# Attention feeding a gated convolution: x and its gate moved into the slot of their own sums, with M held block-diagonal

## Chip, cores and metric

One core of one Trainium2 chip. The metric is the device time of one execution in microseconds, median of several runs. Profiles give a span, which is about 1.8 us shorter than the time of the same run. All runs quoted are in the fast state.

## The reference, cut to what matters

```python
q_pool = q.reshape(B, H, S // 2, 2, D).mean(axis=3)          # B=8, H=8, S=1152, D=64, fp32
attn   = softmax(q_pool @ k.T / sqrt(D))
x      = (attn @ v)                                          # heads joined: (8, 576, 512)
gate   = sigmoid(causal_conv(x, conv_w))                     # 5 taps, per channel
out    = (gate * (x @ w_val)) @ w_out
```

The scores are small, so the kernel takes softmax to first order: attention is then q times a 64x64 matrix M = K'V minus a rank-one term, plus a mean of v. A bound on the scores is computed beside it, and if it fails an exact version runs. No instruction of that version is in the traces.

## The kernel before

32 head pairs are worked in 16 *slots* of two pairs (a, b). A slot sums k and v (`sums`), builds K'V (`grams`), corrects it (`rows`, `rank1`) and reads M out of PSUM. x̂ = Mq, its evacuation to x, the conv (two taps on PE, three on VectorE) and the gate follow **one slot later**, and `val`, `outs` behind them. Cut to the parts concerned:

```python
ps_t: 1 PSUM tile, tag "ts"        # transposes of q AND the sums of k, v share it
ps_g: 1 PSUM tile, tag "g"         # M, and the norms beside it
ps_b: 3 PSUM tiles of two banks    # x̂, conv, val, outs
NOSB = 11                          # output buffers in SBUF; stores are held till all loads are issued

for m in range(NSLOT):
    a, b, pa, pb = 2*m, 2*m+1, 2*m-2, 2*m-1
    sums(a); sums(b); rows(m); grams(a); grams(b)
    tap(pb-2, 1); tap(pb-2, 2)
    xhat(pa); xhat(pb); xevac(pa); xevac(pb)       # of the slot before
    rank1(m); norms(m-1, g); conv(pa); gate(pb-2)
    pool_q(a); stat(m, g); pool_q(b); transposes(a); mk(m, g)
    ...                                            # taps, conv(pb), transposes(b), val/outs
def mk(m, g):      # M for both pairs; each head's M on its own 64 partitions
    nc.scalar.activation(out=mqs[m][:, :, 0:2*D], in_=g[:, 0:256]..., func=AF.Copy, scale=C0)
def xhat(n):       # two halves x two heads, 64x64 matmuls on two row tiles
    nc.tensor.matmul(out=xh[p:p+64, half, 0:HALF], lhsT=mq[p:p+64, i, 0:D], rhs=mq[p:p+64, i, c0:c0+HALF], ...)
def oevac(...):    # copies an output out of PSUM and appends it to `held`
    osb = out_pool.tile([128, m, Dm], FP32, tag=f"osb{m}", bufs=(3 if m == 1 else NOSB))
```

All five instruction streams are ordered by hand: each engine takes its instructions in the order of the program text.

## Time and profile before

| | before |
|---|---|
| median of 4 runs | 187.53 us (186.63 to 188.44) |
| span of the profiled run | 184.8 us |
| busy, PE / VectorE / ScalarE | 88 / 69 / 56 % |
| `rows` of slot 2 / of slot 15 | 35.16 / 153.63 us |
| end of the last matmul | 176.50 us |

How to read it: `rows` is issued once in every slot, so its starts are a clock for the slots. The span falls into three terms: the start up to `rows` of slot 2, the thirteen slots to `rows` of slot 15, and the tail to the last matmul. The prediction below shows the lines.

### The profile page before, as it was taken

The page shows a single profiled execution, that of the slowest core. Times are in us where ns is not written, and L with a number is a line of the kernel's source. Part 1 is how long each engine was busy: PE and PEld are TensorE (multiplying, and loading weights), DVE is VectorE, ACT ScalarE, POOL GpSimd, SP SyncE. Part 2 cuts the span into 40 slices and gives each one's busy share as a digit, 9 for nine tenths or more (in the row PEclk, how much of TensorE's full clock was granted, in tenths as well). Part 3 has the DMA queues.
Part 4 walks back from the last instruction along what each step waited for, and adds up shares of the span by engine and source line. Part 5 has one row for each costly group of instructions (what it writes and reads, how often), then busy time and mean ns, then how long its engine had stood idle before and what let it go on. Part 6 is the DMA issues. An engine that isn't in the chain of part 4 may idle for free.

```text
span 184.8 us, 5451 instructions
## 1 busy us (share of the span) xinstructions
PE 161.8 (88%) x2361; PEld 116.3 (63%) x2361; DVE 127.7 (69%) x236; ACT 102.7 (56%) x151; POOL 75.4 (41%) x118
## 2 busy tenths in 40 slices
PE   7399995699999999999999999999999969969910
PEld 2066752678776868686868667866877648537400
DVE  2162180369889888788888896889788939838550
ACT  2202448075678549754985498549756665494120
POOL 7644434445454455455355444454444345011000
PEclk9969999579999999999999999999999999999995
DMA  5999999999999999999999999999999999953060
GB/s 169 305 207 208 206 207 207 208 207 207 207 206 209 209 205 207 206 208 209 204 208 207 207 209 205 210 203 207 207 208 207 284 419 411 420 231 137 0 274 25
DMA packets 27865, 40.11 MB, mean 217 GB/s; under 512 B 1910, under 2 KB 24758, under 8 KB 27835
## 3 DMA queue, kind: packets, MB, share of 16 engines
q0 software_dynamic: 26624, 36.61, 100.1%
q1 hardware_dynamic: 938, 2.50, 3.8%
q10 hardware_dynamic: 272, 0.59, 0.9%
q8 instruction: 20, 0.33, 0.6%
q14 instruction: 11, 0.08, 0.1%
HBM read 58.73 MB, written 9.44 MB: 369 GB/s over the span
## 4 chain that ended last, share of the span: by engine, by line
DMA 62%; PE 18%; ACT 5%; issue 4%; DVE 3%; POOL 3%; POOLq 0%; DVEq 0%; ACTq 0%
DMA kv<-in_v_dram 33%; DMA qn<-in_q_dram 12%; DMA kv<-in_k_dram 12%; PE vps L329 7%; DMA out_dram<-osb 6%; PE ops L347 3%; PE cps L291 3%; PE g L219 2%; PE sm L209 2%; DVE acc L306 2%; POOL kv L95 2%; ACT osb L360 2%; ACT sq L257 1%; ACT x L275 1%; PE xh L268 1%
## 5 line engine op out<-in xcount | busy, mean ns | idle before, releaser
L306 DVE SCALAR_TENSOR_TENSOR acc<-x,convw_sb,acc 128x576 f32<-128x576 bf16 x62 | 50.6, 816 | 1.5
L347 PE MATMUL ops<-wout_sb,gv 128*128 128x512 bf16 x144 | 34.2, 379 | 1.6 <-ACT osb L360 1.6
L329 PE MATMUL vps<-x,wval_sb 128*128 128x288 bf16 x256 | 34.1, 285 | 1.6 <-ACT osb L360 1.6
L199 ACT COPY mq<-qt_ps 128x576 bf16<-128x576 bf16 x32 | 20.5, 641 | 26.0 <-PE qt_ps L194 26.0
L275 ACT ACTIVATE x<-xh,stats 128x576 bf16<-128x576 f32 x32 | 22.0, 738 | 21.2 <-PE xh L268 21.2
L337 DVE TENSOR_TENSOR gv<-vps,gate 128x576 bf16<-128x576 f32 x32 | 24.1, 757 | 13.5 <-PE vps L329 13.5
L95 POOL DMA_DIRECT2D kv<-in_k_dram x31 | 22.3, 718 | 24.9 <-DMA kv<-in_v_dram 8.5
L99 POOL DMA_DIRECT2D qn<-in_q_dram x31 | 19.8, 639 | 29.4 <-DVE acc L306 10.8
L329 PEld LDWEIGHTS <-wval_sb 128*128 128x128 bf16 x256 | 24.0, 97 | 7.8 <-issue 1.7
L97 POOL DMA_DIRECT2D kv<-in_v_dram x31 | 22.2, 715 | 15.3 <-DMA qn<-in_q_dram 8.9
L301 DVE SCALAR_TENSOR_TENSOR acc<-x,convw_sb,cps 128x576 f32<-128x576 bf16 x31 | 25.1, 810 | 3.6 <-PE cps L291 3.1
L313 ACT ACTIVATE gate<-acc 128x576 bf16<-128x576 f32 x31 | 21.3, 687 | 8.6 <-DVE acc L306 8.6
L291 PE MATMUL cps<-x,diag 128*128 128x288 bf16 x128 | 21.2, 289 | 2.9 <-ACT x L275 2.9
L209 PE MATMUL sm<-kv,first 128*64 128x128 bf16 x576 | 20.5, 226 | 3.6 <-DMA kv<-in_v_dram 3.5
L209 PEld LDWEIGHTS <-first 128*64 128x64 bf16 x576 | 17.4, 113 | 9.3 <-issue 5.2
L347 PEld LDWEIGHTS <-gv 128*128 128x128 bf16 x144 | 13.3, 98 | 14.7 <-issue 1.8
L219 PE MATMUL g<-kv 128*64 128x128 bf16 x576 | 20.4, 228 | 0.0
L257 ACT ACTIVATE sq<-mq 128x1280 bf16<-128x1280 bf16 x16 | 20.2, 1262 | 0.0
L225 DVE TENSOR_TENSOR rows<-sm,rowf 128x256 bf16<-128x256 f32 x16 | 6.8, 425 | 19.4 <-PE sm L209 19.4
L360 ACT COPY osb<-ops 128x1024 f32<-128x1024 f32 (+1 forms) x17 | 15.7, 929 | 7.2 <-PE ops L347 4.2
L219 PEld LDWEIGHTS <-kv 128*64 128x64 bf16 x576 | 18.5, 116 | 0.0
L404 PE MATMUL wps<-idle 128*128 128x512 bf16 x60 | 16.5, 426 | 1.3 <-DVE ident L125 1.3
(65 smaller groups left out, 143.3 us busy)
## 6 DMA issues: line engine op xcount, KB each, us to landing
kv<-in_k_dram POOLq DMA_DIRECT2D x31, 288.0 KB, 10.9
kv<-in_v_dram POOLq DMA_DIRECT2D x31, 288.0 KB, 11.2
qn<-in_q_dram POOLq DMA_DIRECT2D x31, 288.0 KB, 10.9
out_dram<-osb POOLq DMA_DIRECT2D x14, 512.0 KB, 9.8
out_dram<-osb SPq DMA_DIRECT2D x2, 512.0 KB, 2.9
out_dram<-osb POOLq DMA_DIRECT2D x3, 256.0 KB, 9.3
k<-in_k_dram ACTq DMA_DIRECT2D x1, 576.0 KB, 5.7
v<-in_v_dram SPq DMA_DIRECT2D x1, 576.0 KB, 5.1
```

The lines of the kernel that those rows point to most:

```text
L95: nc.gpsimd.dma_start(out=t[:, W:2 * W].rearrange("p (h x) -> p h x", h=2), in_=k[b, h0:h0 + 2].rearrange("h (p t) d -> p h (t d)", p=128))
L97: nc.gpsimd.dma_start(out=t[:, 0:W].rearrange("p (h x) -> p h x", h=2), in_=v[b, h0:h0 + 2].rearrange("h (p t) d -> p h (t d)", p=128))
L209: nc.tensor.matmul(out=sms[m][64 * h:64 * h + 64, i], lhsT=first, rhs=kvv[:, :, h, t, :], start=(i == 0 and t == 0), stop=(t == NT - 1), s ...
L219: nc.tensor.matmul(out=gs[m][64 * h:64 * h + 64, 128 * i:128 * i + 128].rearrange("p (c d) -> p c d", c=2), lhsT=kvv[:, 1, h, t, :], rhs=k ...
L257: nc.scalar.activation(out=sq, in_=mqs[m][:, :, D:], func=AF.Square)
L275: nc.scalar.activation(out=x[:, PAD:].rearrange("p (c n) -> p c n", c=2), in_=xhs.pop(n)[:, :, 0:HALF], func=AF.Identity, bias=stats[:, m, ...
L291: nc.tensor.matmul(out=cps[:, half, 0:HALF], lhsT=w, rhs=x[:, c0:c0 + HALF], start=(i == 0), stop=(i == len(mats) - 1))
L301: nc.vector.scalar_tensor_tensor(out=acc.rearrange("p (c n) -> p c n", c=2), in0=x[:, kk:kk + Sq].rearrange("p (c n) -> p c n", c=2), scal ...
L306: nc.vector.scalar_tensor_tensor(out=accs[n], in0=x[:, kk:kk + Sq], scalar=convw_sb[:, ft, kk:kk + 1], in1=accs[n], op0=ALU.mult, op1=ALU.add)
L329: nc.tensor.matmul(out=vps[:, half, 0:HALF], lhsT=wval_sb[:, fi, ft * 128:(ft + 1) * 128], rhs=x[:, c0:c0 + HALF], start=(fi == 0), stop=( ...
L337: nc.vector.tensor_tensor(out=gvs[y, ft][:, e * Sq:(e + 1) * Sq].rearrange("p (c n) -> p c n", c=2), in0=vps[:, :, 0:HALF], in1=gates.pop( ...
L347: nc.tensor.matmul(out=ops[:, c, :], lhsT=gvs[y, ft][:, t0 + c:t0 + 128 * m:m], rhs=wout_sb[:, ft, :], start=(ft == 0), stop=(ft == NFT - 1))
```

## The change

The intent: q of a slot is pooled and transposed one slot ahead, so that x̂, x, conv and the gate can follow in the same slot as the sums. The pipeline gets one stage shorter, the drain at the end with it, and the time in which PE waits for the first loads gets work. M is written block-diagonally so that x̂ takes four full matmuls; PSUM tiles are taken by number (b0, b1, b2). Cut to its core:

```diff
-    ps_b = ctx.enter_context(tc.tile_pool(name="ps_b", bufs=3, space=PSUM))
+    ps_b = ctx.enter_context(tc.tile_pool(name="ps_b", bufs=1, space=PSUM))   # tags b0, b1, b2
@@ load_pair:  k, v, q  becomes  q, k, v
@@ M
-        nc.scalar.activation(out=mqs[m][:, :, 0:2 * D], in_=g[:, 0:256]..., func=AF.Copy, scale=C0)
+        for h in range(2):            # onto the diagonal of a zeroed 128x128
+            nc.scalar.activation(out=mq2[m % 2][p, :, 64*h:64*h+64], in_=gv[p, :, 0:D], func=AF.Copy, scale=C0)
@@ x̂
-            for h in range(2): nc.tensor.matmul(64x64 ...)
+            nc.tensor.matmul(out=xh[:, half, 0:HALF], lhsT=mq[:, i, 0:2 * D], rhs=mq[:, i, c0:c0 + HALF], ...)
@@ loop
+            sums(a); sums(b); rows(m); grams(a); grams(b)
+            tap(pb, 1); tap(pb, 2)
+        rank1(m); norms(m - 1, g); stat(m, g); mevac(m, g)
+        # even slot
+            gate(pb); gval(bt, 2, val(bt, 2, 0))
+            xhat(a, 1); xhat(b, 2); xevac(a); xevac(b); pool_q(a + 2)
+            gval(bt, 3, val(bt, 3, 0)); transposes(a + 2)
+            conv(a, 1); conv(b, 2); tap(a, 0); pool_q(b + 2); tap(a, 1); tap(a, 2)
+            outs [0]; transposes(b + 2); squares(m, g); gate(a); tap(b, 0); outs [1]; oevac
+        # odd slot
+            outs [0] (or the 1024-row output)
+            xhat(a, 1); xhat(b, 2); xevac(a); xevac(b); pool_q(a + 2)
+            outs [1] (or [0, 1]); oevac
+            conv(a, 1); conv(b, 2); tap(a, 0); transposes(a + 2); pool_q(b + 2)
+            gate(pb); tap(a, 1); tap(a, 2); squares(m, g)
+            gval(bt, 0, val(bt, 0, 0)); transposes(b + 2); gate(a)
+            gval(bt, 1, val(bt, 1, 1)); tap(b, 0)
+            if not moe: warm(20)       # slot 1: filling matmuls, tile b0
```

More of the change, by code (lines that the diff above doesn't have):

```diff
@@ L85, in first_order, with big @@
     ps_g = ctx.enter_context(tc.tile_pool(name="ps_g", bufs=1, space=PSUM))
-    ps_b = ctx.enter_context(tc.tile_pool(name="ps_b", bufs=3, space=PSUM))
+    ps_b = ctx.enter_context(tc.tile_pool(name="ps_b", bufs=1, space=PSUM))
+    def big(name, i):
+        return ps_b.tile([128, 2, 512], FP32, name=name, tag=f"b{i}")
     kvs, loaded = {}, {}
@@ L94, in load_pair @@
         qn = q_pool.tile([QP, 2, 2 * U * D], BF16, name="qn", tag="qn")
+        nc.gpsimd.dma_start(out=qn, in_=q[b, h0:h0 + 2].rearrange("h (p s) d -> p h (s d)", p=QP))
         nc.gpsimd.dma_start(out=t[:, W:2 * W].rearrange("p (h x) -> p h x", h=2),
@@ L98, in load_pair @@
                             in_=v[b, h0:h0 + 2].rearrange("h (p t) d -> p h (t d)", p=128))
-        nc.gpsimd.dma_start(out=qn, in_=q[b, h0:h0 + 2].rearrange("h (p s) d -> p h (s d)", p=QP))
         kvs[n], loaded[n] = t, qn
+    q0 = [q_pool.tile([QP, 2 * U * D], FP32, name="q0", tag="qn") for _ in range(2)]
     k0 = kv_pool.tile([128, 2, NT * D], FP32, name="k0", tag="kv")
     v0 = kv_pool.tile([128, 2, NT * D], FP32, name="v0", tag="kv")
-    q0 = [q_pool.tile([QP, 2 * U * D], FP32, name="q0", tag="qn") for _ in range(2)]
+    for h in range(2):
+        nc.sync.dma_start(out=q0[h], in_=q[0, h].rearrange("(p s) d -> p (s d)", p=QP))
     nc.scalar.dma_start(out=k0, in_=k[0, 0:2].rearrange("h (p t) d -> p h (t d)", p=128))
     nc.sync.dma_start(out=v0, in_=v[0, 0:2].rearrange("h (p t) d -> p h (t d)", p=128))
-    for h in range(2):
-        nc.sync.dma_start(out=q0[h], in_=q[0, h].rearrange("(p s) d -> p (s d)", p=QP))
     wval_sb = consts.tile([128, NFT, Dm], BF16, name="wval_sb")
@@ L160, in setup_conv @@
     def setup_conv():
-        cw_ps = ps_b.tile([128, 2, 512], FP32, name="cw_ps", tag="big")
+        cw_ps = big("cw_ps", 2)
         for ft in range(NFT):
@@ L171, in setup_conv @@
             nc.vector.tensor_scalar_mul(out=diag_l[:, i, :], in0=ident, scalar1=convw_sb[:, NFT - 1, kk:kk + 1])
-    qps, mqs, sqs, gs, sms, rws, xhs = {}, {}, {}, {}, {}, {}, {}
+    mq_pool = ctx.enter_context(tc.tile_pool(name="mqp", bufs=1))
+    mq2 = []
+    for i in range(2):
+        t = mq_pool.tile([128, 2, MQ], BF16, name=f"mq{i}", tag=f"mq{i}")
+        nc.gpsimd.memset(t[0:64, :, D:2 * D], 0.0)
+        nc.gpsimd.memset(t[64:128, :, 0:D], 0.0)
+        mq2.append(t)
+    qps, sqs, gs, sms, rws, xhs = {}, {}, {}, {}, {}, {}
     def pool_q(n):
@@ L186, in pool_q, with transposes @@
         qps[n] = qp
-    def transposes(n):
+    def transposes(n, at=None):
         m, i = divmod(n, 2)
         qp = qps.pop(n)
-        qt_ps = ps_t.tile([128, Sq], BF16, name="qt_ps", tag="ts")
+        qt_ps = (ps_t if at is None else ps_b).tile([128, Sq], BF16, name="qt_ps", tag="ts" if at is None else f"b{at}")
         qtv = qt_ps.rearrange("c (u p) -> c u p", u=U)
@@ L195, in transposes @@
                                 identity=ident[0:QP, 0:QP])
-        if i == 0:
-            mqs[m] = work.tile([128, 2, MQ], BF16, name="mq", tag="mq", bufs=3)
-        nc.scalar.copy(out=mqs[m][:, i, 2 * D:].rearrange("c (p u) -> c p u", u=U),
+        nc.scalar.copy(out=mq2[m % 2][:, i, 2 * D:].rearrange("c (p u) -> c p u", u=U),
                        in_=qt_ps.rearrange("c (u p) -> c p u", u=U))
@@ L249, in stat, with mevac, squares, xhat @@
         nc.vector.tensor_copy(out=stats[:, m, a:z], in_=g[:, 256 + a:256 + z])
-    def mk(m, g):
-        nc.scalar.activation(out=mqs[m][:, :, 0:2 * D], in_=g[:, 0:256].rearrange("p (i c) -> p i c", i=2),
-                             func=AF.Copy, scale=C0)
-    def squares(m):
+    def mevac(m, g):
+        gv = g[:, 0:256].rearrange("p (i c) -> p i c", i=2)
+        for h in range(2):
+            p = slice(64 * h, 64 * h + 64)
+            nc.scalar.activation(out=mq2[m % 2][p, :, 64 * h:64 * h + 64], in_=gv[p, :, 0:D], func=AF.Copy, scale=C0)
+    def squares(m, g):
         sq = work.tile([128, 2, D + Sq], BF16, name="sq", tag="sq")
-        nc.scalar.activation(out=sq, in_=mqs[m][:, :, D:], func=AF.Square)
+        nc.scalar.activation(out=sq[:, :, 0:D], in_=g[:, 0:256].rearrange("p (i c) -> p i c", i=2)[:, :, D:2 * D],
+                             func=AF.Square, scale=C0)
+        nc.scalar.activation(out=sq[:, :, D:], in_=mq2[m % 2][:, :, 2 * D:], func=AF.Square)
         sqs[m] = sq
-    def xhat(n):
+    def xhat(n, at):
         m, i = divmod(n, 2)
-        mq = mqs[m]
-        xh = ps_b.tile([128, 2, 512], FP32, name="xh", tag="big")
+        mq = mq2[m % 2]
+        xh = big("xh", at)
         for half in range(2):
-            for h in range(2):
-                p = 64 * h
-                c0 = 2 * D + half * HALF
-                nc.tensor.matmul(out=xh[p:p + 64, half, 0:HALF], lhsT=mq[p:p + 64, i, 0:D],
-                                 rhs=mq[p:p + 64, i, c0:c0 + HALF], start=True, stop=True, skip_group_check=True)
+            c0 = 2 * D + half * HALF
+            nc.tensor.matmul(out=xh[:, half, 0:HALF], lhsT=mq[:, i, 0:2 * D], rhs=mq[:, i, c0:c0 + HALF],
+                             start=True, stop=True)
         xhs[n] = xh
@@ L279, in first_order, with conv @@
     gates, accs, cpss = {}, {}, {}
-    def conv(n, full=False):
+    def conv(n, at, full=False):
         ft = n % NP
         x = xs[n % NX]
-        cps = ps_b.tile([128, 2, 512], FP32, name="cps", tag="big")
+        cps = big("cps", at)
         mats = [(diag[:, ft, i, :], kk) for i, kk in enumerate(PE_TAPS)]
@@ L321, in first_order, with val @@
     of = out.rearrange("(y b) s d -> y (b s) d", b=2)
-    def val(b, ft):
-        vps = ps_b.tile([128, 2, 512], FP32, name="vps", tag="big")
+    def val(b, ft, at):
+        vps = big("vps", at)
         for fi in range(NFT):
@@ L339, in gval, with outs @@
                                 in1=gates.pop(b * NP + ft).rearrange("p (c n) -> p c n", c=2), op=ALU.mult)
-    def outs(y, t0, m, ops=None, fts=range(4)):
-        if ops is None:
-            ops = ps_b.tile([128, 2, 512], FP32, name="ops", tag="big")
-        for c in range(m):
+    def outs(y, t0, m, ops, cs=None, fts=range(4)):
+        for c in range(m) if cs is None else cs:
             for ft in fts:
@@ L398, in bound_flag, with warm @@
         nc.vector.tensor_scalar(out=flag, in0=fin[:, 3:4], scalar1=lim, scalar2=None, op0=ALU.is_le)
-    def warm(m):
-        wps = ps_b.tile([128, 2, 512], FP32, name="wps", tag="big")
+    def warm(m, at=0):
+        wps = big("wps", at)
         for _ in range(m):
@@ L407, in first_order @@
     warm(12)
+    pool_q(0)
+    transposes(0)
     load_pair(3)
@@ L416, in first_order @@
     nload = 4
-    late = None
     for m in range(NSLOT):
         a, b = 2 * m, 2 * m + 1
-        pa, pb = a - 2, b - 2
-        after = m >= 1
+        pb = b - 2
+        odd = m % 2
         if m == 0:
@@ L424, in first_order @@
             grams(a)
-            pool_q(a)
-            warm(8)
+            pool_q(b)
+            warm(4)
+            transposes(b, 1)
+            warm(4)
             sums(b)
@@ L432, in first_order @@
             sums(b)
-            if late is not None:
-                gval(*late)
-                late = None
             rows(m)
@@ L438, in first_order @@
             grams(b)
-        if m >= 2:
-            tap(pb - 2, 1)
-            tap(pb - 2, 2)
-        if after:
-            xhat(pa)
-            xhat(pb)
-            xevac(pa)
-            xevac(pb)
+            tap(pb, 1)
+            tap(pb, 2)
         rank1(m)
         g = gs.pop(m)
-        if after:
+        if m:
             norms(m - 1, g)
-            conv(pa)
-        if m >= 2:
-            gate(pb - 2)
-        if m:
-            pool_q(a)
-        stat(m, g)
-        pool_q(b)
@@ L458, in first_order @@
-        transposes(a)
-        mk(m, g)
+        stat(m, g)
+        mevac(m, g)
+        if not odd:
+            bt = m // 2 - 1
+            y, e = divmod(bt, 2)
+            moe = bt >= 0
+            if moe:
+                gate(pb)
+                gval(bt, 2, val(bt, 2, 0))
+            else:
+                warm(4)
+            xhat(a, 1)
+            xhat(b, 2)
+            xevac(a)
+            xevac(b)
+            pool_q(a + 2)
+            if moe:
+                gval(bt, 3, val(bt, 3, 0))
+            else:
+                warm(4)
+            transposes(a + 2)
+            conv(a, 1)
+            conv(b, 2)
+            tap(a, 0)
+            pool_q(b + 2)
+            tap(a, 1)
+            tap(a, 2)
+            if moe:
+                ops = big("ops", 0)
+                outs(y, 512 * e, 2, ops, [0])
+            else:
+                warm(6)
+            transposes(b + 2)
+            squares(m, g)
+            gate(a)
+            tap(b, 0)
+            if moe:
+                outs(y, 512 * e, 2, ops, [1])
+                oevac(y, 512 * e, 2, ops)
+            else:
+                warm(6)
+        else:
+            bt = (m - 1) // 2
+            y, e = divmod(bt - 1, 2)
+            moe = bt > 0
+            if moe:
+                if e:
+                    ops = big("ops", 0)
+                    outs(y, 1024, 1, ops)
+                    oevac(y, 1024, 1, ops)
+                else:
+                    ops = big("ops", 0)
+                    outs(y, 256, 2, ops, [0])
+            else:
+                warm(4)
+            xhat(a, 1)
+            xhat(b, 2)
+            xevac(a)
+            xevac(b)
+            if m + 1 < NSLOT:
+                pool_q(a + 2)
+            if moe:
+                if e:
+                    ops = big("ops", 0)
+                outs(y, 256 + 512 * e, 2, ops, [0, 1] if e else [1])
+                oevac(y, 256 + 512 * e, 2, ops)
+            else:
+                warm(4)
+            conv(a, 1)
+            conv(b, 2, full=m + 1 == NSLOT)
+            tap(a, 0)
+            if m + 1 < NSLOT:
+                transposes(a + 2)
+                pool_q(b + 2)
+            gate(pb)
+            tap(a, 1)
+            tap(a, 2)
+            squares(m, g)
+            if m + 1 == NSLOT:
+                gate(b)
+            gval(bt, 0, val(bt, 0, 0))
+            if m + 1 < NSLOT:
+                transposes(b + 2)
+            gate(a)
+            gval(bt, 1, val(bt, 1, 1))
+            if m + 1 < NSLOT:
+                tap(b, 0)
+            if not moe:
+                warm(20)
@@ L465, in first_order @@
                 store(*held.pop(0), nc.gpsimd)
-        if m < 2:
-            warm(6)
-            if after:
-                tap(pa, 0)
-                conv(pb)
-            warm(6)
-            transposes(b)
-            if after:
-                tap(pa, 1)
-                tap(pa, 2)
-                gate(pa)
-                tap(pb, 0)
-            squares(m)
-            warm(8)
-        elif m % 2 == 0:
-            bt = m // 2 - 1
-            tap(pa, 0)
-            if bt:
-                y, e = divmod(bt - 1, 2)
-                oevac(y, 256 + 512 * e, 2, outs(y, 256 + 512 * e, 2))
-            conv(pb)
-            tap(pa, 1)
-            tap(pa, 2)
-            if bt and e:
-                oevac(y, 1024, 1, outs(y, 1024, 1))
-            transposes(b)
-            gate(pa)
-            vps = val(bt, 0)
-            tap(pb, 0)
-            gval(bt, 0, vps)
-            squares(m)
-            late = (bt, 1, val(bt, 1))
-        else:
-            bt = (m - 1) // 2 - 1
-            y, e = divmod(bt, 2)
-            v2 = val(bt, 2)
-            tap(pa, 0)
-            gval(bt, 2, v2)
-            v3 = val(bt, 3)
-            gval(bt, 3, v3)
-            tap(pa, 1)
-            tap(pa, 2)
-            conv(pb)
-            transposes(b)
-            gate(pa)
-            squares(m)
-            o = outs(y, 512 * e, 2)
-            tap(pb, 0)
-            oevac(y, 512 * e, 2, o)
@@ L517, in first_order @@
-    m, bt = NSLOT, B - 1
-    pa, pb = 2 * m - 2, 2 * m - 1
-    xhat(pa)
-    xhat(pb)
-    tap(pb - 2, 1)
-    tap(pb - 2, 2)
-    xevac(pa)
-    xevac(pb)
-    y, e = divmod(bt - 1, 2)
-    o = outs(y, 256 + 512 * e, 2)
-    conv(pa)
-    tap(pa, 0)
-    gate(pb - 2)
-    conv(pb, full=True)
-    oevac(y, 256 + 512 * e, 2, o)
-    tap(pa, 1)
-    tap(pa, 2)
-    g = ps_g.tile([128, 512], FP32, name="g", tag="g")
-    norms(m - 1, g, start=True)
-    gate(pb)
-    gate(pa)
-    while held:
-        store(*held.pop(0), nc.gpsimd)
@@ L540, in first_order @@
-    for ft in range(NFT):
-        gval(bt, ft, val(bt, ft))
-    stat(m, g)
+    g = ps_g.tile([128, 512], FP32, name="g", tag="g")
+    norms(NSLOT - 1, g, start=True)
+    gval(bt, 2, val(bt, 2, 0))
+    gval(bt, 3, val(bt, 3, 2))
+    stat(NSLOT, g)
     bound_reduce()
     y, e = divmod(bt, 2)
-    o1 = outs(y, 512, 2, fts=range(3))
-    o2 = outs(y, 768, 2, fts=range(3))
-    outs(y, 512, 2, o1, [3])
+    o1, o2, o3 = big("ops", 1), big("ops", 0), big("ops", 2)
+    outs(y, 512, 2, o1, fts=range(3))
@@ L548, in first_order @@
+    outs(y, 768, 2, o2, fts=range(3))
+    outs(y, 512, 2, o1, fts=[3])
     oevac(y, 512, 2, o1, nc.sync)
     bound_sums()
-    outs(y, 768, 2, o2, [3])
+    outs(y, 768, 2, o2, fts=[3])
     oevac(y, 768, 2, o2, nc.sync)
     bound_flag()
-    oevac(y, 1024, 1, outs(y, 1024, 1), nc.sync)
+    outs(y, 1024, 1, o3)
+    oevac(y, 1024, 1, o3, nc.sync)
 def exact_softmax(ctx, tc, q, k, v, moe_w_val, moe_conv_w, moe_w_out, out):
```

## The prediction

> **What bounds the kernel now.** I read the page first, then the timeline of the start, a table of busy time by stretch, the timeline of VectorE in one slot, and last the chain that ended last.
>
> The page's second part, 40 slices of 4.62 us:
>
> ```profile
> PE   7399995699999999999999999999999969969910
> ...
> PEclk9969999579999999999999999999999999999995
> DMA  5999999999999999999999999999999999953060
> ```
>
> PE and the DMA engines are both full to about slice 35. To find which of them sets the pace, look at who waits. In the timeline of the start PE waits for a load once, in front of slot 2 (a slot is one pass of the loop, two head pairs):
>
> ```profile
> 33.94 1.17 PE L209 MATMUL sm<-kv,first 128*64 128x128 bf16 x18 [3.51 <-DMA kv<-in_v_dram]
> ...
> 35.16 0.43 DVE L225 TENSOR_TENSOR rows<-sm,rowf 128x256 bf16<-128x256 f32 x1 [7.45 <-PE sm L209]
> ```
>
> Up to there the kernel is bound by loads. Behind it the VectorE op on line 225 (`rows`, one per slot) is a clock for the slots. Taking stretches from one `rows` to the next, slots 5 to 12:
>
> ```profile
> 61.78:70.47 8.69, 8.53 (x150) 6.54 (x146) 7.50 (x12) 4.56 (x8) 4.28 (x7) 1.00 1.20 208
> 70.47:80.14 9.67, 9.40 (x154) 6.94 (x150) 7.73 (x13) 8.12 (x12) 4.42 (x7) 1.00 1.19 207
> ...
> sum 71.71, PE 70.01 PEld 53.11 DVE 60.89 ACT 49.53 POOL 34.15; mean PE 8.75 PEld 6.64 DVE 7.61 ACT 6.19 POOL 4.27
> ```
>
> The columns are length, then PE, PEld, DVE, ACT, POOL busy. A slot lasts 8.96 us in the mean and PE is busy for 98% of it, VectorE for 85%. So from 34 us on PE is the bound, and VectorE has 1.35 us to spare. Loads come at 6 x 1.42 = 8.5 us per slot (288 KB in bf16, at 207 GB/s), a little faster than PE takes them. The stores are held until every load is issued. The chain shows where that bites, in slot 14:
>
> ```profile
> 138.94 10.24 DMA out_dram<-osb
> ...
> 149.27 1.02 ACT osb L360
> ```
>
> The first store lands at 149.2, right behind the last load, and the twelfth two-row `osb` (there are 11 buffers) waits for it.
>
> **What the Trainium skill says.** (1) "PSUM — Partial Sum Buffer", section "PSUM bank collisions raise a hardware error": two engines must not touch the same bank and quadrant at once, reads included. In both kernels the build has ScalarE's read of M out of the tile `g` wait on VectorE, whose only access to `g` is `stat`. So M waits for `stat`; before, that cost nothing, for M was used a slot later. (2) The same page, "Engine vs sequencer instructions": VectorE's queue is strict FIFO. The trace agrees: VectorE stands 0.3 us in front of a `gv` while later ops could run. (3) "ScalarE: Activation LUTs", "What ACT_TABLE_LOAD costs": an ACTIVATE costs 186 ns + 0.833 ns per element of the free dimension. The trace has 404 ns for M (128x256) where this gives 399; I estimate from it 0.29 us for each half of M. (4) "TensorE: Matmul & The Clock Gate", Part 1: an idle window of about 3.4 us halves the clock. The trace agrees: the wait of 3.51 us above is followed by slices with a clock of 0.5 and 0.7.
>
> **The change part by part.**
>
> *Block-diagonal M.* x̂ goes from 8 matmuls 64x288 a slot (issued in 0.38 us, for two row tiles run side by side) to 4 of 128x288 (4 x 0.12 = 0.49). Against +0.1 us PE saves nothing. ScalarE gets one more op for M and one for the squares, 0.3 us a slot of some 2.5 free.
>
> *A slot earlier, one chain.* x, conv and gate of a pair now come in the slot of its sums. VectorE's order in a slot is now (from the built order): rows, two taps of the slot before, stat, [gval], pool_q, [gval], tap 0 of pair a, pool_q, two taps, [odd: gval, gval], tap 0 of pair b. With durations from the timeline and neighbours overlapping 0.08, from R = start of `rows`:
> rows and taps end at R+2.01, stat R+2.10; two halves of M on ScalarE to R+2.62; x̂ on PE from 2.66, the first half usable at 3.11; x on ScalarE (0.74) to 3.85; conv on PE. Odd slots without the 1024-row output: PE first finishes half an output (0.9), conv at 4.06, result at 4.76. VectorE has only pool_q meanwhile and idles from 2.57 to 4.76. Then tap 0, pool_q, two taps, two gvals, tap 0 of b: 0.73+0.47+1.59+0.68+0.68+0.73, next `rows` at R+9.63. Where the 1024-row output is added (slots 5, 9, 13) PE has 0.9 more in front of conv: 10.53. Even slots fill the gap with a gval, pool_q and the other gval; PE is the limit there and reaches the next `rows` at R+8.84 (rank1 waits for rows, norms, val, x̂ at 2.66, val, transpose, two conv, outs, transpose, outs, sums 1.24). So four slots take 2 x 8.84 + 9.63 + 10.53 = 37.8, or 9.46 a slot in place of 8.96: VectorE becomes the bound in odd slots. From `rows` of slot 2 to that of slot 15: 7 x 8.84 + 3 x 9.63 + 3 x 10.53 = 122.4; before 35.16 to 153.63 = 118.5. **+3.9 us.**
>
> *Start.* The work of slot 1 now fills the time in which PE waited, which is the intent. But VectorE's pool_q of pair 5 stands ahead of the taps of pair 2 and of gval 0, and q of pair 5 comes 2 transfers before v of pair 5, which itself moves back by one: 33.9 + 1.4 − 2.8 = 32.5. Then pool_q 0.55, taps 1.67, gval 0.76: 35.4. Only then may the 20 warm matmuls reuse their PSUM tile: 20 x 0.216 = 4.3 to 39.8, and up to 2 more at a halved clock, likely after some 3 us of idle PE. I take slot 2's sums at 41.0, its `rows` at 42.2 in place of 35.16. **+7.0 us.**
>
> *End.* From the last `rows` to the end of the last matmul took 22.9 us (153.63 to 176.50), for a whole stage of slot 15 was still to come. Now: conv of both pairs done at R+5.8, four val and the norms to 10.05 (gated by gval), 20 outs and the two sums 5.1: 15.15. **−7.7 us.** The last evacuation and store stay as they are.
>
> Sum: +7.0 + 3.9 − 7.7 = **+3.2 us** on a span of 184.8. On the median of 188.33 that makes **191.5 us**.
>
> **The rivals.** (a) *The drain of the pipeline is pure gain*: work moves into the idle start, the tail is 8 us shorter, slots stay at 8.96: −5 us or more. For it: PE was idle or warming in slots 0 to 2. Against it: the osb wait. The change now evacuates an output in slots 2 and 3, so the twelfth osb falls in slot 13, not 14, while the first store cannot land before 149.2, since the DMA engines are full until then. From that osb on remain 5 us of slot 13, two slots and the tail. Even with slots at PE's own pace (8.8) that is 1.0 + 2.3 + 8.8 + 8.9 + 7.0 = 28 us: last matmul at 177.2, against 176.5. So whatever is gained earlier is lost in that wait; a gain over 2% is hardly possible. This rival makes about 188.5 us.
> (b) *VectorE's gaps are worse than I draw them*: each handover costs a little more and even slots don't recover; +0.3 us in each of 14 slots, +4 more: about 196.
> (c) *The warm matmuls don't cost*: the clock stays full, slot 2 begins at 39.5; then the osb wait takes 0.5 to 1 back: about 190.5.
>
> **Range and chances.** The osb floor holds the low side at about +0.7 us by (a), the unseen waits open the high side: 188 to 196. Faster by over 2% needs a span under 181, against the floor: 0.05. The limit of slower by 2% is +3.8 us, just above my sum: 0.42. Within: 0.53.
>
> **What would show it.** `rows` of slot 2 near 42 and slots of 8.8 (even), 9.6 and 10.5 (odd); VectorE idle about 2 us before tap 0 in odd slots, waiting for conv; PE below 95% there; the first store landing near 149 and the osb of slot 13 waiting for it little or not at all; last `rows` to last matmul near 15 us. I am wrong if odd slots are as long as before, if slot 2 starts by 37, or if loads end well before 148, so that the osb floor falls.

## More of the kernel before

The fast runs of the kernel before still fall into two groups, near 186.7 and 188.4 us, here and in all later rounds; what sets them apart was not looked into. Its profile is of the faster group.

## The result, and the profile after

| | before | after |
|---|---|---|
| median | 187.53 us (4 runs) | 193.57 us (193.11 to 195.12, 4 runs) |
| ratio of fast runs | | 1.0337, 95% interval 1.0246 to 1.0427: slower |
| span | 184.8 | 191.3 |
| `rows` of slot 2 | 35.16 | 40.92 (+5.8) |
| `rows` of slot 2 to slot 15 | 118.5 | 127.1 (+8.6) |
| last `rows` to end of last matmul | 22.9 | 15.0 (−7.9) |

A ratio is the mean time of one kernel's fast runs over that of the other's of the same rounds, so not quite the ratio of the medians. The three terms add to +6.5 us, the difference of the spans.

**Start.** The timeline of the changed kernel (start, length, engine, line, operation; in brackets the idle time before and what ended it), from the pooling of q of pair 5 to `rows` of slot 2:

```profile
32.41 0.56 DVE L198 TENSOR_TENSOR qp<-qn 96x768 bf16<-96x768 bf16 x1 [0.34 <-DMA qn<-in_q_dram]
...
35.27 4.48 PE L414 MATMUL wps<-idle 128*128 128x512 bf16 x19 [0.83 <-DVE gv L349]
39.68 1.20 PE L219 MATMUL sm<-kv,first 128*64 128x128 bf16 x36
...
40.92 0.42 DVE L235 TENSOR_TENSOR rows<-sm,rowf 128x256 bf16<-128x256 f32 x1 [4.31 <-PE sm L219]
```

q landed at 32.4, the filling matmuls waited for a `gv` (their tile b0 had to be read), and then ran 4.4 us in front of the sums of slot 2.

**Slots.** The same table by stretch as for the kernel before (length; PE, PEld, DVE, ACT, POOL busy), from `rows` to `rows`: a plain odd slot, an even one, an odd one with the 1024-row output, and the sum of slots 2 to 11:

```profile
50.17:60.04 9.87, 8.78 (x146) 6.51 (x143) 7.40 (x12) 7.72 (x13) 4.49 (x8) 1.00 1.19 208
60.04:69.30 9.26, 8.86 (x144) 6.27 (x141) 7.58 (x13) 5.24 (x10) 4.75 (x7) 1.00 1.19 207
69.30:80.12 10.82, 9.59 (x150) 6.86 (x147) 7.40 (x13) 8.32 (x14) 4.87 (x7) 1.00 1.19 207
...
sum 97.79, PE 89.97 PEld 64.57 DVE 74.83 ACT 65.98 POOL 45.03; mean PE 9.00 PEld 6.46 DVE 7.48 ACT 6.60 POOL 4.50
```

PE is busy for 92% (89.97 of 97.79), where it was 98% (slots 5 to 12): a slot lasts 0.82 us longer in the mean (9.78 against 8.96), and only 0.25 of that is busy time of PE (9.00 against 8.75). Where PE and VectorE stand is seen in the plain odd slot from 50.17. VectorE:

```profile
52.18 0.54 DVE L198 TENSOR_TENSOR qp<-qn 96x768 bf16<-96x768 bf16 x1
55.03 0.81 DVE L313 SCALAR_TENSOR_TENSOR acc<-x,convw_sb,cps 128x576 f32<-128x576 bf16 x1 [2.31 <-PE cps L303]
...
59.14 0.81 DVE L313 SCALAR_TENSOR_TENSOR acc<-x,convw_sb,cps 128x576 f32<-128x576 bf16 x1
60.04 0.42 DVE L235 TENSOR_TENSOR rows<-sm,rowf 128x256 bf16<-128x256 f32 x1
```

It idles 2.31 us in front of tap 0, waiting for conv, and then works without a break up to the next `rows`: that is the step the prediction drew. (`tap 0` is the first of VectorE's three conv taps, the one that reads conv out of PSUM.) ScalarE and PE at the end of the same slot:

```profile
57.07 1.16 ACT L271 ACTIVATE sq<-mq 128x1152 bf16<-128x1152 bf16 x1
58.12 0.64 ACT L209 COPY mq<-qt_ps 128x576 bf16<-128x576 bf16 x1
...
58.81 1.20 PE L219 MATMUL sm<-kv,first 128*64 128x128 bf16 x36 [0.72 <-ACT mq L209]
```

The sums of the next slot wait 0.72 us for ScalarE's copy of the second transposes. The prediction did not see this wait: both live in the one PSUM tile "ts", and the copy stands behind the squares in ScalarE's queue. The sums end at 60.01, so in this slot PE's chain and VectorE's reach `rows` at 60.04 together; e1 parts the two.

**Output buffers and tail.** In slot 13 the twelfth two-row osb is written at 153.24 and waits for PE alone and for no store, as the slots were late enough. That line, the last `rows` and the last matmuls:

```profile
153.24 1.01 ACT L370 COPY osb<-ops 128x1024 f32<-128x1024 f32 x1 [0.70 <-PE ops L357]
...
168.04 0.42 DVE L235 TENSOR_TENSOR rows<-sm,rowf 128x256 bf16<-128x256 f32 x1 [0.21 <-PE sm L219]
...
181.55 1.47 PE L357 MATMUL ops<-wout_sb,gv 128*128 128x512 bf16 x6
```

### The profile page after: what moved, and what is told of

Its sections match the earlier page's. It is cut to its first block, busy times and chain, and to the rows that moved or that the text cites. A ratio compares the mean times of both kernels' runs of the same rounds, so it can differ in the third digit from the quotient of the medians.

```text
span 191.3 us, 5379 instructions
## 1 busy us (share of the span) xinstructions
PE 165.8 (87%) x2286; PEld 113.0 (59%) x2305; DVE 125.9 (66%) x236; ACT 109.0 (57%) x183; POOL 77.3 (40%) x122
## 4 chain that ended last, share of the span: by engine, by line
PE 45%; DVE 21%; DMA 12%; ACT 12%; POOL 3%; issue 3%; DVEq 0%; ACTq 0%; POOLq 0%
PE ops L357 10%; PE vps L341 10%; PE sm L219 9%; DVE acc L318 7%; DMA qn<-in_q_dram 7%; DMA kv<-in_k_dram 5%; DVE gv L349 5%; PE cps L303 4%; ACT mq L209 4%; ACT sq L271 3%; PE g L229 3%; DVE acc L313 3%; PE xh L280 3%; PE qt_ps L207 3%; ACT mq L265 2%
## 5 line engine op out<-in xcount | busy, mean ns | idle before, releaser
L341 PE MATMUL vps<-x,wval_sb 128*128 128x288 bf16 x256 | 36.5, 285 | 0.3
L357 PE MATMUL ops<-wout_sb,gv 128*128 128x512 bf16 x129 | 35.2, 379 | 0.8
L265 ACT ACTIVATE mq<-g 64x128 bf16<-64x128 f32 x32 | 8.7, 272 | 33.4 <-DVE stats L259 33.2
L219 PE MATMUL sm<-kv,first 128*64 128x128 bf16 x576 | 19.8, 223 | 6.0 <-ACT mq L209 4.7
L414 PE MATMUL wps<-idle 128*128 128x512 bf16 x64 | 19.9, 452 | 2.7 <-DVE ident L129 1.4
L229 PE MATMUL g<-kv 128*64 128x128 bf16 x576 | 19.6, 222 | 0.0
L364 POOL DMA_DIRECT2D out_dram<-osb x17 | 9.1, 539 | 24.3 <-ACT osb L370 15.9
L271 ACT ACTIVATE sq<-mq 128x1152 bf16<-128x1152 bf16 x16 | 18.6, 1166 | 0.0
L303 PE MATMUL cps<-x,diag 128*128 128x288 bf16 x128 | 18.5, 285 | 0.0
L229 PEld LDWEIGHTS <-kv 128*64 128x64 bf16 x576 | 17.7, 112 | 0.0
## 6 DMA issues: line engine op xcount, KB each, us to landing
qn<-in_q_dram POOLq DMA_DIRECT2D x31, 288.0 KB, 10.9
```

What stands on the lines that cost most here:

```text
L219: nc.tensor.matmul(out=sms[m][64 * h:64 * h + 64, i], lhsT=first, rhs=kvv[:, :, h, t, :], start=(i == 0 and t == 0), stop=(t == NT - 1), s ...
L229: nc.tensor.matmul(out=gs[m][64 * h:64 * h + 64, 128 * i:128 * i + 128].rearrange("p (c d) -> p c d", c=2), lhsT=kvv[:, 1, h, t, :], rhs=k ...
L271: nc.scalar.activation(out=sq[:, :, D:], in_=mq2[m % 2][:, :, 2 * D:], func=AF.Square)
L303: nc.tensor.matmul(out=cps[:, half, 0:HALF], lhsT=w, rhs=x[:, c0:c0 + HALF], start=(i == 0), stop=(i == len(mats) - 1))
L341: nc.tensor.matmul(out=vps[:, half, 0:HALF], lhsT=wval_sb[:, fi, ft * 128:(ft + 1) * 128], rhs=x[:, c0:c0 + HALF], start=(fi == 0), stop=( ...
L357: nc.tensor.matmul(out=ops[:, c, :], lhsT=gvs[y, ft][:, t0 + c:t0 + 128 * m:m], rhs=wout_sb[:, ft, :], start=(ft == 0), stop=(ft == NFT - 1))
```

## The experiments

All ten kernels gave correct results. Ratios are against the kernel before, run in the same rounds; the changed kernel itself stands at 1.0337.

**e1, squares late.** In odd slots of the changed kernel:

```diff
-            squares(m, g)                          # ahead of val 0
             gval(bt, 0, val(bt, 0, 0))
             transposes(b + 2)
+            squares(m, g)
```

> The changed kernel, in odd slots squares after the transposes of the second pair, so that the copy of those transposes no longer stands behind squares in ScalarE's queue. Theory T (a shared PSUM tile: the sums of the next slot reuse the tile of the transposes and wait for ScalarE's copy, 0.7 to 0.9 us before every even slot): that wait goes, sums of even slots start about 0.9 earlier, the norms and val behind them 0.4 earlier, and each pair of slots is 0.3 to 0.4 us shorter, 2 us in all: span near 189.2. Theory V (VectorE's order alone bounds odd slots, by the 2.3 us that it waits for conv): VectorE has no idle time before rows of even slots already, so at most 0.2 us per pair of slots is gained, span 190 to 191.3.

Measured: ratio 1.0203 (1.0149 to 1.0256), 191.34 us, span 188.9. Plain odd slots take 9.69, those with the 1024-row output 10.66, even ones behind them 9.03 to 9.04, one 9.30. Of an odd slot with the 1024-row output: the sums no longer wait for the copy:

```profile
76.61 0.64 ACT L209 COPY mq<-qt_ps 128x576 bf16<-128x576 bf16 x1
...
77.49 1.20 PE L219 MATMUL sm<-kv,first 128*64 128x128 bf16 x36
...
79.49 0.41 DVE L235 TENSOR_TENSOR rows<-sm,rowf 128x256 bf16<-128x256 f32 x1
```

The sums have ended at 78.69, 0.8 us ahead of `rows`, which now waits for VectorE alone. The shared tile is real and worth 2.3 us between `rows` of slot 2 and of slot 15. Theory V did not fall with it, for odd slots are still long.

**e2, no filling matmuls.** `if not moe: warm(20)` is taken out.

> The changed kernel without the 20 filling matmuls at the end of slot 1. Theory W (these matmuls, which can start only when gval 0 has freed their PSUM tile, hold back slot 2 by 4.4 us past the landing of its load at about 35.3): rows of slot 2 near 36.5 in place of 40.92, span lower by 4.4, less up to 1 us that the twelfth osb in slot 13 then waits for the first store: 187 to 188. Rival (without them the clock falls to half for a window or two, as it does before, at a cost of about 3 us): rows of slot 2 near 36.5 to 37, but slot 2 some 2 to 3 us longer, span 189 to 190.5.

Measured: ratio 1.0088 (1.0038 to 1.0138), 189.42 us, span 187.6; `rows` of slot 2 at 36.51, slot 2 itself 9.03: no clock loss. ScalarE in slot 13:

```profile
149.88 1.01 ACT L370 COPY osb<-ops 128x1024 f32<-128x1024 f32 x1 [2.00 <-DMA out_dram<-osb]
```

Of 4.4 us gained at the start 3.7 arrive; that slot is 11.73 in place of 10.82. The osb wait comes back as soon as slot 13 comes earlier.

**e3, the kernel before with 13 output buffers.** `NOSB = 11` becomes 13.

> The kernel before with 13 output buffers in place of 11. If the wait of the twelfth osb for the first store is on the path that sets the end (ScalarE waits 2.9 us in slot 14 and PE 1.6 us in front of vps, then 1.6 in front of ops in slot 15), the span falls by 2 to 3 us, to 182 to 183, and the last matmul ends near 174. If the wait only took up slack, the span stays at 184.8. In either case it tells how much of the distance between the two kernels the osb wait hides.

Measured: ratio 0.9864 (0.981 to 0.9918), 185.52 us, span 183.9; `rows` of slot 2 to that of slot 15 116.2 in place of 118.5. The wait was on the path, and two buffers take some 2.5 us off the kernel before by the ratio. The span fell by 0.9 only, above the 182 to 183 expected, because in this profiled run PE was slower in the tail:

```profile
161.34 3.33 PE L347 MATMUL ops<-wout_sb,gv 128*128 128x512 bf16 x8 [1.61 <-ACT osb L360]
```

The same eight matmuls took 1.89 us in the profile of the kernel before, and the page of e3 shows a granted clock of 0.6 in that slice. From the last `rows` to the last matmul it took 24.55 in place of 22.87.

**e4, x̂ on row tiles again.** The changed kernel with x̂ from the diagonal blocks:

```diff
-            nc.tensor.matmul(out=xh[:, half, 0:HALF], lhsT=mq[:, i, 0:2 * D], rhs=mq[:, i, c0:c0 + HALF], ...)
+            for h in range(2):
+                nc.tensor.matmul(out=xh[p:p + 64, half, 0:HALF], lhsT=mq[p:p + 64, i, p:p + 64], rhs=mq[p:p + 64, i, ...])
```

> The changed kernel with xhat as before: eight 64x64 matmuls a slot on two row tiles, taking the diagonal blocks of M, in place of four full ones. My prediction says that the full ones save PE nothing (0.49 against 0.38 us of issue a slot): here 0 to 1.5 us lower, span 189.8 to 191.3. If changing the tiling drains TensorE, as the Trainium skill says under TensorEngine Tiling (Array Packing), Key Properties, the two more changes per slot cost 0.1 to 0.3 us each slot: span 192.5 to 195.

Measured: ratio 1.0321 (1.027 to 1.0372), 193.75 us, span 191.9; even slots 9.25, plain odd ones 9.98 against 9.87. The span met neither expectation (it lies between them), and in time the two forms can't be told apart. The run changes x̂'s form and the tiling together, so it doesn't time a change of tiling alone. The block-diagonal M is not where the time went, nor a gain.

**e5, pool_q in the gap.** e1 with 13 output buffers (no osb waits for a store in e1, so they should change nothing), and from slot 2 on:

```diff
             xevac(a); xevac(b)
             pool_q(a + 2)
+            pool_q(b + 2)
             ...
             tap(a, 0)
-            pool_q(b + 2)
```

> e1_squares_late (span 188.9) with 13 output buffers, and with pool_q of the second pair right behind pool_q of the first, in VectorE's gaps, in every slot from 2 on. The work is the same. Theory V (VectorE's order bounds odd slots: it waits 2.3 us for conv, 3.3 where the 1024-row output is added, with pool_q still to do behind): odd slots lose 0.47 us each, from 9.69 and 10.66 to about 9.2 and 10.2. In even slots the second transposes no longer wait for pool_q, 0.24 us each of 9.03. Together 4 to 4.5 us, span near 184.6. Rival (the gap is only the shadow of PE, which bounds the slot by its own chain of val, xhat and conv): slots as in e1, span 188.5 to 189. The two more buffers should do nothing in e1, where the twelfth osb comes after the first store.

Measured: ratio 0.9985 (0.993 to 1.004), 187.06 us, span 185.2. Plain odd slots 9.42, with the 1024-row output 10.33, even ones 8.78. VectorE in the same odd slot as above:

```profile
52.02 1.01 DVE L198 TENSOR_TENSOR qp<-qn 96x768 bf16<-96x768 bf16 x2
54.87 0.81 DVE L313 SCALAR_TENSOR_TENSOR acc<-x,convw_sb,cps 128x576 f32<-128x576 bf16 x1 [1.84 <-PE cps L303]
```

The same work in another order makes odd slots 0.3 shorter: VectorE's order bounds them. Even slots gain 0.25.

**e6, stat ahead of the taps.** e1 with 13 output buffers, and in odd slots `stat` moved ahead of `tap(pb, 1); tap(pb, 2)`.

> e1_squares_late with 13 output buffers, and in odd slots stat ahead of the two taps of the slot before, so that M and xhat start earlier and the taps lie in the gap. stat must then wait for the norms (about 1.65 us after rows, in place of 1.9). Theory V: M comes 0.25 to 0.3 us earlier, conv and tap 0 as much, odd slots 9.4 and 10.4, six of them: span 187.2. If the latency from rows to conv isn't on the path: 188.9.

Measured: ratio 1.0111 (1.0058 to 1.0163), 189.51 us, span 186.9; odd slots 9.34 and 10.41. As theory V has it: the latency from `rows` to conv is on the path.

**e7, all three taken away.** e5 without the filling matmuls.

> e5_pools_gap without the 20 filling matmuls: all three causes taken away at once. If the terms add, the span is that of e5 less 4.4 us, near 180.2, which beats both kernels by over 2%; rows of slot 2 at 36.5, the first store at 149, no osb wait with 13 buffers. Rival: with slots of 9.4 in the mean slot 15 starts earlier than its last load lands (v of pair 31 near 148): rows of slot 15 at 36.5 + 118.5 = 155 lies behind that, so the loads shouldn't bind.

Measured: ratio 0.9757 (0.9711 to 0.9803), 183.00 us, span 181.4; `rows` of slot 2 at 36.49. That is 1.2 us above what was expected: e5 itself came 0.6 higher, and with slot 2 earlier pool_q, now ahead of conv, waits for its load in the first slots (2.22 us in slot 3, which takes 9.74).

**e8, loads in the order k, v, q.** The changed kernel with the `dma_start` of q moved behind those of k and v.

> The changed kernel with the loads of a pair in the order of before (k, v, q). Theory of the start: q of pair 5 lands 2 transfers later (35.2 in place of 32.4), pool_q of pair 5, the taps and gval 0 behind it and the 20 filling matmuls all move by 2.8 us: rows of slot 2 near 43.7, span near 194.1, slots as long as before. Rival (v, which now lands a transfer earlier, counts for more): rows of slot 2 at 39.5 to 41, span 190 to 191.5.

Measured: ratio 1.0573 (1.0509 to 1.0636), 198.29 us, span 194.9; `rows` of slot 2 at 44.51 (+3.6), the same slots. That is 0.8 later than expected: PE stood idle for 2.65 us before the last transposes of slot 1, and the val behind them took 2.12 in place of 1.15, so the clock had halved. q first is a part of the change that pays: q of pair 5, not v, starts the chain that ends in slot 2.

**e9, the gap filled further.** e7 with, in odd slots:

```diff
-            rows; tap(pb, 1); tap(pb, 2); stat; pool_q(a + 2); pool_q(b + 2); tap(a, 0)      # VectorE's order
+            rows; pool_q(a + 2); stat; tap(pb, 1); tap(pb, 2); pool_q(b + 2); tap(a, 0)
```

> e7_pools_nowarm (span 181.4) with the odd slots' VectorE gap filled further: pool_q of the first pair ahead of stat, stat ahead of the two taps, pool_q of the second pair behind them. Theory V: rows to conv gets 0.3 us shorter and 0.5 us less work lies behind tap 0, odd slots 8.9 and 9.8 in place of 9.42 and 10.32, then bound by PE (8.85 by its own chain): six slots by 0.5, span near 178.4. If the odd slots are already bound by PE, or the loads (8.58 us a slot) get in the way in the first slots: 180 to 181.4.

Measured: ratio 0.9658 (0.9614 to 0.9703), 181.11 us, span 179.1. From slot 3 on even slots take 8.8, plain odd ones 9.05, those with the 1024-row output 10.07; that is 0.15 and 0.27 above the expected 8.9 and 9.8, and the span 0.7 above its 178.4. VectorE in a plain odd slot:

```profile
84.31 0.18 DVE L259 COPY stats<-g 128x22 f32<-128x22 f32 x1 [0.67 <-PE g L254]
84.41 1.66 DVE L318 SCALAR_TENSOR_TENSOR acc<-x,convw_sb,acc 128x576 f32<-128x576 bf16 x2
85.99 0.55 DVE L198 TENSOR_TENSOR qp<-qn 96x768 bf16<-96x768 bf16 x1
87.26 0.81 DVE L313 SCALAR_TENSOR_TENSOR acc<-x,convw_sb,cps 128x576 f32<-128x576 bf16 x1 [0.73 <-PE cps L303]
```

The gap of 2.31 us is split into 0.67 and 0.73 and the slot is 0.37 shorter than in e7, 0.8 shorter than in the changed kernel. This is the best version: 3.4% ahead of the kernel before, and 2.1% ahead of e3 by the two ratios.

**e10, e7 with 11 output buffers.**

> e7_pools_nowarm with the 11 output buffers that both kernels have, in place of 13. My prediction's claim (a): the twelfth osb (slot 13) can't be written before the first store lands, near 149.5, and whatever is gained ahead of it is lost there. rows of slot 13 in e7 is at 139.0 and the osb would be written about 5 us later, so it waits 5 us: span near 186, as long as the kernel before. If the wait takes up slack only, as ScalarE has some: under 183.

Measured: ratio 1.0172 (1.0122 to 1.0221), 190.98 us, span 188.8, 7.4 us above e7. ScalarE and PE in slot 13:

```profile
149.71 1.01 ACT L370 COPY osb<-ops 128x1024 f32<-128x1024 f32 x1 [6.30 <-DMA out_dram<-osb]
```

```profile
150.77 2.08 PE L341 MATMUL vps<-x,wval_sb 128*128 128x288 bf16 x8 [5.45 <-ACT osb L370]
```

The osb waits for the first store to 149.7 (149.27 before, 149.88 in e2), and everything gained ahead of it is lost. It costs more than the 5 us expected: PE idle for 5.45 us finds its clock halved (2.08 us for a val that takes 1.15), and the next val takes 2.07.

## Why the prediction was right, and where its sum was off

The time, 193.57, lies in the range of 188 to 196, and the main mechanism held: VectorE's gap in odd slots, a late slot 2 and a shorter tail were all there. The size was off: +3.2 us was expected and the spans differ by +6.5, twice as much. That 191.5 came within 2 us is in part luck. It was added to 188.33, a time of the slower group of the kernel before, while the span of 184.8 belongs to the run of 186.63; from there it makes 189.8 against 193.11. Also the start was drawn 1.2 us too long, which hid part of the 4.7 us missing in the slots. And the likeliest outcome named, within 2% (0.53), did not come; slower by more had 0.42. Step by step, predicted against measured:

- **Start, +7.0 against +5.8.** The chain is as drawn: q of pair 5 at 32.4 (32.5 predicted), the taps, a `gv`, then the filling matmuls. e2 takes 4.4 us of it away, e8 adds 3.6. The clock stayed full: the filling matmuls ended at 39.68 (39.8 predicted), so the 1.2 us allowed for a halved clock were the error.
- **Slots, +3.9 against +8.6: the mis-sized term.** It is 13 slots from `rows` of slot 2. Odd slots were drawn at 9.63 and 10.53 and measured 9.87 and 10.82; even ones at 8.84 and measured 9.25, one 9.52. What failed is the step that in an even slot "PE is the limit there and reaches the next `rows` at R+8.84": it starts from sums that are already done when `rows` comes. They were late, because the sums share a PSUM tile with the transposes of q and waited up to 0.9 us for a copy queued behind the squares. With late sums `rank1` begins at R+0.90, where in e1 it begins at R+0.47, and the second val, which must wait until a `gv` has read its PSUM tile, at R+3.45 against R+3.23: these 0.22 us are what an even slot loses. e1 removes that wait and 2.3 of the 4.7 us that were missing, and then odd slots measure 9.69 and 10.66, within 0.13 of the drawing. The other 2.4 us lie mostly in even slots at 9.03: there the second transposes wait some 0.25 us for pool_q, and e5, which ends that wait, brings them to 8.78. So even slots from slot 4 on are accounted for; the one of 9.52 and the last 0.1 us of the odd ones were not taken apart.
- **VectorE's gap** in odd slots was predicted at 2.2 us and measured 2.31. That it bounds the slot is shown by e5, e6 and e9: reordering alone, with no work removed, shortens plain odd slots by 0.27 and 0.35 (e5 and e6, over e1) and by another 0.37 (e9, over e7).
- **End, −7.7 against −7.9.** Right, and outweighed nearly twice by the other two terms.
- **Block-diagonal M.** Called no gain for PE; e4 finds none, and no loss either. The 0.1 us a slot that I put against it came of a misreading: before, the eight row-tile matmuls of x̂ held PE from 62.67 to the next op at 63.19, which is 0.52 us and not 0.38; now the four full ones hold it from 52.91 to 53.41, 0.50.
- **Rival (a)**, the output buffers. In the changed kernel as it stands they don't bind. As a floor under any improvement of it the claim is shown: where slot 13 comes earlier the wait is 2.0 us in e2 and 6.3 in e10, and e10 with a span of 188.8 is slower than the kernel before. It is a floor for 11 buffers only: with 13, e9 beats the kernel before by 3.4%. The floor was even drawn too low, as the halved clock behind the wait was left out.
- **Rival (b)**, more at each handover, is near to what came, but its cause was not general looseness: half of it is one PSUM tile.
- **Rival (c)**, no halved clock, was right about the clock (the sums of slot 2 began at 39.68, 39.5 predicted) but not about the sum.

So the gain that was to be expected was there (7.9 us in the tail). It went into longer slots and into a late slot 2.

## What to carry to other kernels

Taking a stage out of a pipeline turns a dependence that had a slot to resolve into a latency inside the slot. On engines that take work in order, look at what stands *behind* the op that now waits, and put independent work ahead of it: moving pool_q took the span from 188.9 to 185.2 (e1 to e5). When PSUM or SBUF buffers are shared between uses, count the queue that their reader stands in, and when part of a kernel gets faster, look for the buffer (here the twelfth output tile) that ties it to a fixed event.

## What the Trainium skill lacked or had wrong

- "TensorEngine Tiling (Array Packing)", Key Properties, says that changing the tiling mode drains TensorE and gives no cost. Two more changes a slot, together with x̂'s other form (e4), left even slots as they were and made plain odd ones 0.11 us longer, with no measurable difference in time (1.0321 against 1.0337). The cost of one change by itself was not measured.
- "DMA: Bandwidth & Descriptors", Anatomy of one DMA — SWDGE (gpsimd) path: its fit of 2.0 us + bytes/436e3 is for each DMA by itself. With the queue kept full, a load of 288 KB landed 10.9 us after its issue in the median, and the first store 10.2 us after its own, with loads still landing. I found the queued case, which set the osb wait here, on no page.
- "PSUM — Partial Sum Buffer" tells one to guard PSUM by bank and quadrant; that a shared tile also ties an engine to everything queued ahead of its reader (0.72 us here, 2.3 in all) is on no page that I found.
